# Another way to turn 32 columns of x0: VectorE instead of TensorE in a cross-network kernel, and fewer, larger loads

## The chip, the cores and the metric

The kernel runs on one core of one Trainium2 chip. The metric is device time in microseconds (us) for one execution, as the median of several runs; lower is better. A profile is one further execution, recorded by the hardware profiler. Its "span" is the stretch from the first to the last recorded instruction, and the execution's own time is a little longer than that.

The engines are named as the profile names them: PE is TensorE (matmuls), PEld its weight loads, DVE is VectorE, ACT is ScalarE, POOL is GpSimd, SP is SyncE, which only issues DMAs. ACTq and SPq are the DMA issues of ACT and SP.

## The reference

```
x0: (4096, 416) bf16,  ws: (6, 416, 416) bf16,  bs: (6, 416) bf16

def reference(x0, ws, bs):
    x = x0
    for l in range(ws.shape[0]):
        x = x0 * (x @ ws[l] + bs[l]) + x
    return x
```

Six layers, each a matmul of 4096 x 416 with 416 x 416, a bias, an elementwise product with x0 and a sum with the layer's input.

## The kernel before

**Layout.** Layers 0 to 4 work on transposed data: features lie on the 128 partitions, rows of the batch on the free axis. The 416 features are three blocks of 128 (`XM`, index `m` or `k`) and a remainder of 32. The 4096 batch rows are two halves (`s` = 0, 1) of 2048, and each half is four groups (`g`) of 512 columns. The remainder's 32 features would fill only a quarter of the partitions, so the four groups of a half are stacked: in `XR`, partitions 32g to 32g+31 hold the 32 features of group g, in 512 columns for each half. `XRd` is `XR` with its upper and lower 64 partitions exchanged; layer 0 reads it for the block m = 1 so that neighbouring matmuls use different rows of TensorE.

**Getting x0 there.** The three main blocks come from memory by DMA transposes (L75, `load_x0t`, one for each half and group, eight in all, on SP's queue). The remainder comes as plain rows of 64 bytes. For half 0 four loads on ScalarE's queue (L80) put them into `xrig`, ordered so that four 128 x 128 transposes on TensorE (L155, against the identity) give the stacked form in PSUM, from where VectorE copies it to `XR` and `XRd` (L158). For half 1 one load on SP's queue (L84) fetches them into `xrem`, GpSimd copies them into the order that `xrig` needs (L132), and TensorE and VectorE do the same as for half 0, with the spare bank of the tile `pr` as target.

**The order around it.** SP issues, one after the other: the x0 transposes of half 0, that of half 1's group 0, `xrem` (L84, called at L114), the other three of half 1, then the weights of layers 1 to 5, the batch rows of x0 for the last layer (`X0rows`, L123, four loads), and the last layer's bias row for four partitions (`bLr`, L125, four loads). ScalarE's queue issues the weights of layer 0, the biases, the `xrig` loads and the remainder's weights of layer 0 (`WR`, L87). ScalarE then copies those weights to further partitions (L108) and begins the activations.

**Layer 0** is `first_layer(s)`, half 0 and then half 1. TensorE's matmuls of the main blocks are L212, those of the remainder rows L219 (into the same sums), those that make the remainder's own output L191 and L196. Each block's two groups of 512 columns share a PSUM tile of two banks; four such tiles exist, and ScalarE frees one when it has read it. `ew_main` is: ScalarE adds the bias while it reads PSUM (L163), VectorE multiplies by x0 (L164) and adds the layer's input (L167). `ew_rem` does the same for the remainder (L171, L172, L173). `x0_rem(1, ...)` is called between half 0's `mm_rem` and the elementwise work on half 0's second pair of groups.

**Layers 1 to 4** are the loop at L280 (matmuls L179, L185, L191, L196, the same elementwise work). **Layer 5** computes with the batch rows on the partitions (L325, L331, L334): ScalarE takes the sum out of PSUM (L352), VectorE multiplies by `X0rows` (L353) and adds (L342), and the result is stored (L343).

A planner of the framework lays out each engine's instructions in the order of a planned time and inserts the waits. `tc.keep_in_program_order(ins)` ties one instruction behind the instruction that was written before it for the same engine.

Of the kernel before, what the change touches and what calls it, by code (L numbers as in the profile page):

```python
# [11 lines left out]
BF16 = mybir.dt.bfloat16  # L12
# [4 lines left out]
def kernel(  # L17
# [7 lines left out]
    nc = tc.nc  # L25
    B, D = x0.shape
    L = ws.shape[0]
    P = 128
    NK = 3
    R = D - NK * P  # L30
    assert R == 32 and B == 4096 and D == 416 and L >= 2
    NS = 2
    NG = 4
    CW = 512
    SW = NG * CW
    NBT = B // P
    LL = L - 1

    const = ctx.enter_context(tc.tile_pool(name="const", bufs=1))
    big = ctx.enter_context(tc.tile_pool(name="big", bufs=1))  # L40
# [4 lines left out]
    x0_v = x0.rearrange("(bt p) d -> p bt d", p=P)  # L45
    out_v = out.rearrange("(bt p) d -> p bt d", p=P)

    ident = const.tile([P, P], BF16)
# [6 lines left out]
    bLr = const.tile([P, D], BF16)  # L55
    bM = const.tile([P, NK, L], FP32)
    bR = const.tile([P, L], FP32)
    X0rows = big.tile([P, NBT, D], BF16)
    XLrows = big.tile([P, NBT, D], BF16)
    scrR = [big.tile([P, 4, P], BF16, name=f"scrR{s}") for s in range(NS)]  # L60
    xrem = big.tile([P, 16, R], BF16)
    xrig = big.tile([P, NS, 4, P], BF16)
    XRd = big.tile([P, NS * CW], BF16)
    XM = [big.tile([P, NK, B], BF16, name=f"XM{i}") for i in range(3)]
    XR = [big.tile([P, NS * CW], BF16, name=f"XR{i}") for i in range(3)]

    def col0(s, g):
        return SW * s + CW * g

    def load_wm(eng, l):  # L70
        eng.dma_start(WM[:, l], ws[l, 0:NK * P, :].rearrange("(k p) n -> p k n", p=P))

    def load_x0t(s, g):
        c0 = col0(s, g)
        nc.sync.dma_start_transpose(out=XM[0][:, :, c0:c0 + CW], in_=x0[c0:c0 + CW, 0:NK * P])  # L75

    def load_xrem0():
        with nc.allow_non_contiguous_dma(reason="64B row segments"):
            for i in range(4):
                nc.scalar.dma_start(xrig[:, 0, i, :].rearrange("p (g r) -> p g r", g=NG), x0_v[:, i:16:4, NK * P:D])  # L80

    def load_xrem1():
        with nc.allow_non_contiguous_dma(reason="64B row segments"):
            nc.sync.dma_start(xrem[:], x0_v[:, 16:32, NK * P:D])  # L84

    def load_wr0():
        nc.scalar.dma_start(WR[0:R, 0, :], ws[0, NK * P:D, :])  # L87
# [12 lines left out]
    nc.scalar.dma_start(bsb[:], bs[:, :])  # L100
    load_x0t(0, 1)
    load_xrem0()
    load_wr0()
    nc.scalar.activation(dz[:, 1:2], dz[:, 0:1], ACT.Identity, bias=dz[:, 0:1], scale=1.0)  # L104
    for g in range(1, NG):
        dst, src = WR[32 * g:32 * g + 32, 0, :], WR[0:R, 0, :]
# [4 lines left out]
    for g in range(2, NG):  # L111
        load_x0t(0, g)
    load_x0t(1, 0)
    load_xrem1()  # L114
    for g in range(1, NG):
        load_x0t(1, g)
    load_wm(nc.sync, 1)
# [1 line left out]
        load_wr(nc.sync, g, 1, L)  # L119
    for l in range(2, L):  # L120
        load_wm(nc.sync, l)
    for q in range(4):
        nc.sync.dma_start(X0rows[:, 8 * q:8 * q + 8, :], x0_v[:, 8 * q:8 * q + 8, :])  # L123
    for g in range(NG):
        nc.sync.dma_start(bLr[32 * g:32 * g + 1, :], bs[LL:LL + 1, :])  # L125

    def fill_wd(l0, l1):
        for g in range(NG):
            nc.gpsimd.tensor_copy(WD[32 * g:32 * g + 32, l0:l1, g, :], WR[32 * g:32 * g + 32, l0:l1, NK * P:D])

    fill_wd(0, 1)
    nc.gpsimd.tensor_copy(xrig[:, 1].rearrange("p i (g r) -> p i g r", g=NG), xrem[:].rearrange("p (g i) r -> p i g r", g=NG))  # L132
    fill_wd(1, L)

    wps = psum.tile([P, CW], FP32, tag="ps", name="wps")
# [14 lines left out]
        nc.vector.tensor_copy(bM[:], pb[:, 0:NK, 0:L])  # L150
        nc.vector.tensor_copy(bR[:], pb[:, 3, 0:L])

    def x0_rem(s, tpr):
        for i in range(4):
            nc.tensor.transpose(tpr[:, 128 * i:128 * i + 128], xrig[:, s, i, :], ident[:])  # L155
        for dst, src in ((slice(0, P), slice(0, P)), (slice(64, P), slice(0, 64)), (slice(0, 64), slice(64, P))):
            to = XR[0] if dst == src else XRd
            nc.vector.tensor_copy(to[dst, CW * s:CW * s + CW], tpr[src])  # L158

    def ew_main(l, s, m, h, pt, cur, nxt, pin=False):  # L160
        c0 = col0(s, 2 * h)
        t = tpool.tile([P, 2 * CW], BF16, name="t")
        nc.scalar.activation(t[:], pt[:].rearrange("p a b -> p (a b)"), ACT.Identity, bias=bM[:, m, l:l + 1], scale=1.0)  # L163
        prod = nc.vector.tensor_tensor(out=t[:], in0=t[:], in1=XM[0][:, m, c0:c0 + 2 * CW], op=ALU.mult)  # L164
        if pin:
            tc.keep_in_program_order(prod)
        nc.vector.tensor_tensor(out=nxt[:, m, c0:c0 + 2 * CW], in0=t[:], in1=cur[:, m, c0:c0 + 2 * CW], op=ALU.add)  # L167

    def ew_rem(l, s, pr, curR, nxtR):
        tr = tpool.tile([P, 2 * CW], BF16, name="t")  # L170
        nc.scalar.activation(tr[:, 0:CW], pr, ACT.Identity, bias=bR[:, l:l + 1], scale=1.0)  # L171
        nc.vector.tensor_tensor(out=tr[:, 0:CW], in0=tr[:, 0:CW], in1=XR[0][:, CW * s:CW * s + CW], op=ALU.mult)  # L172
        nc.vector.tensor_tensor(out=nxtR[:, CW * s:CW * s + CW], in0=tr[:, 0:CW], in1=curR[:, CW * s:CW * s + CW], op=ALU.add)  # L173
# [15 lines left out]
    def mm_rem(l, s, pr, cur, curR):  # L189
        for g in range(NG):  # L190
            nc.tensor.matmul(pr[32 * g:32 * g + 32, :], lhsT=WD[:, l, g, :], rhs=curR[:, CW * s:CW * s + CW],  # L191
                             start=True, stop=False, tile_position=(0, 32 * g))
        for k in range(NK):
            for g in range(NG):
                c0 = col0(s, g)
                nc.tensor.matmul(pr[32 * g:32 * g + 32, :], lhsT=WM[:, l, k, NK * P:D], rhs=cur[:, k, c0:c0 + CW],  # L196
                      start=False, stop=(k == NK - 1), tile_position=(0, 32 * g))
# [8 lines left out]
    def first_layer(s):  # L206
        cur, curR, nxt, nxtR = XM[0], XR[0], XM[1], XR[1]

        def full(pt, m, h, gl, after_row):
            c0 = col0(s, 2 * h + gl)  # L210
            for k in range(NK):
                nc.tensor.matmul(pt[:, gl, :], lhsT=WM[:, 0, k, 128 * m:128 * m + 128], rhs=cur[:, k, c0:c0 + CW],  # L212
                                 start=(k == 0 and not after_row), stop=(k == NK - 1 and after_row))

        def row(pt, m, h, opens):
            for gl in range(2):
                rg = 32 * ((2 * h + gl) ^ (2 if m == 1 else 0))
                src = XRd if m == 1 else curR
                nc.tensor.matmul(pt[:, gl, :], lhsT=WR[rg:rg + 32, 0, 128 * m:128 * m + 128],  # L219
                                 rhs=src[rg:rg + 32, CW * s:CW * s + CW],  # L220
                                 start=opens, stop=not opens, tile_position=(rg, 0))

        def ph(m):
            return psum.tile([P, 2, CW], FP32, tag="ps", name=f"ph{m}")

        pa = [ph(m) for m in range(NK)]
        if s == 0:
            for m in range(NK):
                full(pa[m], m, 0, 0, False)
            tp0 = psum.tile([P, CW], BF16, tag="ps", name="tpr")  # L230
            x0_rem(0, tp0[:])
            for m in range(NK):
                full(pa[m], m, 0, 1, False)
        else:
            for m in range(NK):
                for gl in range(2):
                    full(pa[m], m, 0, gl, False)
        pb = [ph(0)]
        row(pa[0], 0, 0, False)
        row(pb[0], 0, 1, True)  # L240
        row(pa[2], 2, 0, False)
        row(pa[1], 1, 0, False)
        for m in range(NK):
            ew_main(0, s, m, 0, pa[m], cur, nxt)
        for m in range(NK):
            if m:
                pb.append(ph(m))
            for gl in range(2):
                full(pb[m], m, 1, gl, m == 0)
        row(pb[1], 1, 1, False)  # L250
        row(pb[2], 2, 1, False)
        pr = psum.tile([P, 2, CW], FP32, tag="ps", name="pr")
        mm_rem(0, s, pr[:, 0, :], cur, curR)
        if s == 0:
            x0_rem(1, pr[:, 1, :].bitcast(BF16)[:, 0:CW])
        for m in range(NK):
            ew_main(0, s, m, 1, pb[m], cur, nxt, pin=(s == 0))
        ew_rem(0, s, pr[:, 0, :], curR, nxtR)
# [3 lines left out]
    for s in range(NS):  # L262
        first_layer(s)
# [147 lines left out]
```

## Time and profile before

| | us |
|---|---|
| median of 3 runs | 130.65 (130.53 to 130.75) |
| the profiled execution's own time | 130.58 |
| its span | 128.8 |

| engine | busy us | share of the span | instructions |
|---|---|---|---|
| PE | 123.6 | 96% | 1691 |
| DVE | 106.7 | 83% | 195 |
| ACT | 86.9 | 67% | 99 |
| POOL | 6.2 | 5% | 18 |

The granted TensorE clock is 1.00 throughout. The DMA engines are busy in the first 40 us (x0 and the weights come in) and in the last 28 us (results go out).

How to read what follows. A row of the timeline is: start in us, length in us, engine, line, operation, what it writes and reads, how many; in brackets the engine's idle time just before it and what ended it. Rows of the same kind are merged. Matmuls overlap, so their length in the profile (0.38 us for 512 columns) is longer than the distance from one start to the next (0.216 us); starts are the surer reading. A row of the chain of waits is: start, length, and the work that the end of the execution goes back to at that moment.

### The profile page before, as it was taken

How to read it: one execution, taken by the hardware profiler on the slowest of the kernel's cores; microseconds unless marked ns; L12 is line 12 of the kernel's file. 1: busy time of each engine (PE TensorE's matmuls, PEld its weight loads, DVE VectorE, ACT ScalarE, POOL GpSimd, SP SyncE). 2: the span in 40 equal slices, each digit the busy share in tenths (PEclk: the TensorE clock that was granted, in tenths of full speed). 3: DMA queues.
4: the chain of work that ended last, by engine and by line, in shares of the span. 5: the costliest groups of instructions: out<-in, count | busy, mean ns of one | idle time of the engine just before them, and what ended most of it. 6: DMA issues, size and time to landing. Idle time of an engine off the chain costs nothing.

```text
span 128.8 us, 3973 instructions
## 1 busy us (share of the span) xinstructions
PE 123.6 (96%) x1691; PEld 55.1 (43%) x1691; DVE 106.7 (83%) x195; ACT 86.9 (67%) x99; POOL 6.2 (5%) x18
## 2 busy tenths in 40 slices
PE   7999999999999999999999999999999999999960
PEld 3343443344545444434444544444444445445420
DVE  0023989999999898989898989898989899898991
ACT  0138873887848667848668848668858896569670
POOL 4004300600000000000000000000000000000000
PEclk9999999999999999999999999999999999999999
DMA  4999999999990000000000000000297999985754
GB/s 95 244 231 207 163 153 264 253 328 333 336 291 9 5 0 8 0 0 5 0 5 0 5 0 5 0 5 0 45 163 169 119 237 191 217 261 186 235 178 138
DMA packets 42102, 16.37 MB, mean 127 GB/s; under 512 B 30906, under 2 KB 42084, under 8 KB 42084
## 3 DMA queue, kind: packets, MB, share of 16 engines
q1 hardware_dynamic: 39368, 15.53, 53.9%
q10 hardware_dynamic: 2716, 0.59, 2.5%
q8 instruction: 13, 0.21, 0.7%
q14 instruction: 5, 0.04, 0.1%
HBM read 6.15 MB, written 3.41 MB: 74 GB/s over the span
## 4 chain that ended last, share of the span: by engine, by line
PE 89%; DVE 6%; issue 2%; ACT 1%; DVEq 0%
PE pt L179 49%; PE ph L212 13%; PE py L325 8%; PE pt L185 5%; PE pr L196 5%; PE wps L139 4%; DVE t L353 4%; DVE o L342 2%; PE pr L191 2%; PE ph L219 1%; PE py L331 1%; PE py L334 1%; ACT t L352 1%; PE tpr L155 0%; PE pr L155 0%
## 5 line engine op out<-in xcount | busy, mean ns | idle before, releaser
L179 PE MATMUL pt<-XM,WM 128*32 128x512 bf16 x1152 | 65.2, 379 | 0.0
L163 ACT ACTIVATE t<-pt,bM 128x1024 bf16<-128x1024 f32 x48 | 49.6, 1115 | 18.5 <-PE pt L185 18.5
L164 DVE TENSOR_TENSOR t<-t,XM 128x1024 bf16<-128x1024 bf16 x60 | 41.4, 690 | 5.2 <-ACT t L163 5.2
L167 DVE TENSOR_TENSOR XM<-t,XM 128x1024 bf16<-128x1024 bf16 x60 | 41.8, 697 | 3.4
L179 PEld LDWEIGHTS <-WM 128*32 128x32 bf16 x1152 | 29.7, 97 | 33.8 <-issue 5.1
L352 ACT CAST t<-py 128x416 bf16<-128x416 f32 (+1 forms) x23 | 14.8, 642 | 4.8 <-PE py L325 2.6
L325 PE MATMUL py<-WM,XM 128*128 128x416 bf16 x96 | 17.7, 340 | 0.0
L212 PE MATMUL ph<-XM,WM 128*128 128x512 bf16 x72 | 16.5, 381 | 0.0
L163 ACT ACTIVATE t<-ph,bM 128x1024 bf16<-128x1024 f32 x12 | 12.5, 1114 | 3.4 <-PE ph L219 3.4
L325 PEld LDWEIGHTS <-XM 128*128 128x128 bf16 x96 | 9.0, 98 | 8.5 <-issue 1.4
L353 DVE TENSOR_TENSOR t<-t,X0rows 128x416 bf16<-128x416 bf16 (+1 forms) x23 | 10.4, 457 | 1.2 <-ACT t L352 1.2
L342 DVE TENSOR_TENSOR o<-t,XLrows 128x416 bf16<-128x416 bf16 (+1 forms) x23 | 10.4, 456 | 0.0
L212 PEld LDWEIGHTS <-WM 128*128 128x128 bf16 x72 | 6.7, 98 | 8.4 <-issue 1.1
L171 ACT ACTIVATE t<-pr,bR 128x512 bf16<-128x512 f32 x10 | 6.4, 685 | 2.7 <-PE pr L196 2.1
L196 PE MATMUL pr<-XM,WM 128*32 128x512 bf16 x120 | 8.2, 379 | 0.0
L185 PE MATMUL pt<-XR,WR 32*128 32x512 bf16 x96 | 7.3, 379 | 0.0
L139 PE MATMUL wps<-const-bfloat16-1.0 128*128 128x512 bf16 (+1 forms) x12 | 4.9, 592 | 0.8 <-PEq L395 0.8
L104 ACT ACT_TABLE_LOAD x1 | 1.3, 1283 | 6.0 <-DMA XM<-in_x_dram 6.0
L173 DVE TENSOR_TENSOR XR<-t,XR 128x512 bf16<-128x512 bf16 x10 | 4.2, 425 | 0.7
L196 PEld LDWEIGHTS <-WM 128*32 128x32 bf16 x120 | 3.2, 97 | 3.0
L150 DVE CAST bM<-pb 128x18 f32<-128x18 bf16 x1 | 0.2, 177 | 5.1 <-PE pb L149 5.1
L172 DVE TENSOR_TENSOR t<-t,XR 128x512 bf16<-128x512 bf16 x10 | 4.2, 420 | 0.0
(38 smaller groups left out, 33.5 us busy)
## 6 DMA issues: line engine op xcount, KB each, us to landing
X0rows<-in_x_dram SPq DMA_DIRECT2D x4, 832.0 KB, 11.5
out_dram<-o SPq DMA_DIRECT2D x9, 208.0 KB, 2.5
WM<-in_ws_dram SPq DMA_DIRECT2D x5, 312.0 KB
out_dram<-o SPq DMA_DIRECT2D x13, 104.0 KB, 1.9
WR<-in_ws_dram SPq DMA_DIRECT2D x4, 130.0 KB, 4.1
WM<-in_ws_dram ACTq DMA_DIRECT2D x1, 312.0 KB
XM<-in_x_dram SPq DMA_TRANSPOSE x8, 4.9
xrig<-in_x_dram ACTq DMA_DIRECT2D x4, 32.0 KB, 4.2
```

The source lines that it names most:

```text
L139: nc.tensor.matmul(wps[:, 0:cols], lhsT=warm[:, 0:P], rhs=warm[:, 0:cols], start=True, stop=True)
L163: nc.scalar.activation(t[:], pt[:].rearrange("p a b -> p (a b)"), ACT.Identity, bias=bM[:, m, l:l + 1], scale=1.0)
L164: prod = nc.vector.tensor_tensor(out=t[:], in0=t[:], in1=XM[0][:, m, c0:c0 + 2 * CW], op=ALU.mult)
L167: nc.vector.tensor_tensor(out=nxt[:, m, c0:c0 + 2 * CW], in0=t[:], in1=cur[:, m, c0:c0 + 2 * CW], op=ALU.add)
L179: nc.tensor.matmul(pts[g // 2][32 * q:32 * q + 32, g % 2, :], lhsT=WM[:, l, k, 128 * m + 32 * q:128 * m + 32 * q + 32], rhs=cur[:, k, c0:c ...
L185: nc.tensor.matmul(pts[g // 2][:, g % 2, :], lhsT=WR[32 * g:32 * g + 32, l, 128 * m:128 * m + 128], rhs=curR[32 * g:32 * g + 32, CW * s:CW ...
L196: nc.tensor.matmul(pr[32 * g:32 * g + 32, :], lhsT=WM[:, l, k, NK * P:D], rhs=cur[:, k, c0:c0 + CW], start=False, stop=(k == NK - 1), tile ...
L212: nc.tensor.matmul(pt[:, gl, :], lhsT=WM[:, 0, k, 128 * m:128 * m + 128], rhs=cur[:, k, c0:c0 + CW], start=(k == 0 and not after_row), sto ...
L325: nc.tensor.matmul(py[:, 0:D], lhsT=cur[:, k, q_cols(q, g)], rhs=WM[:, l, k, :], start=((not closes) and k == 0), stop=(closes and k == NK ...
L342: tc.keep_in_program_order(nc.vector.tensor_tensor(out=o, in0=t, in1=xl, op=ALU.add))
L352: nc.scalar.copy(tv, src)
L353: tc.keep_in_program_order(nc.vector.tensor_tensor(out=tv, in0=tv, in1=X0rows[:, b, :], op=ALU.mult))
```

## The change

The remainder of half 1 no longer goes through GpSimd and TensorE. Its load takes the rows in another order (sixteen neighbouring rows on each partition), so that one VectorE transpose in blocks of 32 x 32 writes the stacked form straight to `XR`; two copies inside the on-chip memory make `XRd`. The load moves from SP's queue to ScalarE's and is called after half 0's remainder is done: a small memset of `xrem` on VectorE, tied behind the copies of half 0, must be over before the load may write there, and the load itself is tied behind what stands before it on ScalarE's queue. `xrig` serves half 0 alone. `X0rows` comes in one load instead of four, `bLr` in one load with a repeated source instead of four.

```
+    def pin(ins):
+        tc.keep_in_program_order(ins)
...
     def load_xrem1():
+        pin(nc.vector.memset(xrem[:, 0, 0:1], 0.0))
         with nc.allow_non_contiguous_dma(reason="64B row segments"):
-            nc.sync.dma_start(xrem[:], x0_v[:, 16:32, NK * P:D])
+            pin(nc.scalar.dma_start(xrem[:], x0[SW:2 * SW, NK * P:D].rearrange("(p t) r -> p t r", p=P)))
...
     load_x0t(1, 0)
-    load_xrem1()
     for g in range(1, NG):
         load_x0t(1, g)
...
-    for q in range(4):
-        nc.sync.dma_start(X0rows[:, 8 * q:8 * q + 8, :], x0_v[:, 8 * q:8 * q + 8, :])
-    for g in range(NG):
-        nc.sync.dma_start(bLr[32 * g:32 * g + 1, :], bs[LL:LL + 1, :])
+    nc.sync.dma_start(X0rows[:], x0_v)
+    nc.sync.dma_start(bLr[0:P:32, :], bs[LL:LL + 1, :].to_broadcast([NG, D]))
...
-    nc.gpsimd.tensor_copy(xrig[:, 1].rearrange("p i (g r) -> p i g r", g=NG), xrem[:].rearrange("p (g i) r -> p i g r", g=NG))
...
-    def x0_rem(s, tpr):
+    def x0_rem0(tpr):
         for i in range(4):
-            nc.tensor.transpose(tpr[:, 128 * i:128 * i + 128], xrig[:, s, i, :], ident[:])
+            nc.tensor.transpose(tpr[:, 128 * i:128 * i + 128], xrig[:, i, :], ident[:])
         for dst, src in ((slice(0, P), slice(0, P)), (slice(64, P), slice(0, 64)), (slice(0, 64), slice(64, P))):
             to = XR[0] if dst == src else XRd
-            nc.vector.tensor_copy(to[dst, CW * s:CW * s + CW], tpr[src])
+            pin(nc.vector.tensor_copy(to[dst, 0:CW], tpr[src]))
+        load_xrem1()
+
+    def x0_rem1():
+        pin(nc.vector.transpose(XR[0][:, CW:2 * CW].rearrange("p (j t) -> p t j", t=16), xrem[:]))
+        for dst, src in ((slice(64, P), slice(0, 64)), (slice(0, 64), slice(64, P))):
+            pin(nc.vector.tensor_copy(XRd[dst, CW:2 * CW], XR[0][src, CW:2 * CW]))
...
         if s == 0:
-            x0_rem(1, pr[:, 1, :].bitcast(BF16)[:, 0:CW])
+            x0_rem1()
```

More of the change, by code (lines that the diff above doesn't have):

```diff
@@ L61 @@
     xrem = big.tile([P, 16, R], BF16)
-    xrig = big.tile([P, NS, 4, P], BF16)
+    xrig = big.tile([P, 4, P], BF16)
     XRd = big.tile([P, NS * CW], BF16)
@@ L79, in load_xrem0 @@
             for i in range(4):
-                nc.scalar.dma_start(xrig[:, 0, i, :].rearrange("p (g r) -> p g r", g=NG), x0_v[:, i:16:4, NK * P:D])
+                nc.scalar.dma_start(xrig[:, i, :].rearrange("p (g r) -> p g r", g=NG), x0_v[:, i:16:4, NK * P:D])
     def load_xrem1():
+        pin(nc.vector.memset(xrem[:, 0, 0:1], 0.0))
         with nc.allow_non_contiguous_dma(reason="64B row segments"):
-            nc.sync.dma_start(xrem[:], x0_v[:, 16:32, NK * P:D])
+            pin(nc.scalar.dma_start(xrem[:], x0[SW:2 * SW, NK * P:D].rearrange("(p t) r -> p t r", p=P)))
     def load_wr0():
@@ L230, in first_layer @@
             tp0 = psum.tile([P, CW], BF16, tag="ps", name="tpr")
-            x0_rem(0, tp0[:])
+            x0_rem0(tp0[:])
             for m in range(NK):
```

## The prediction

> **What bounds the kernel now.** I read the chain of waits first. It is TensorE without a break from 0.77 us to 115.65 us of the span, and after that a short ScalarE step and VectorE to the end:
>
> ```profile
> 15.41 0.33 PE ph L219 x4
> 15.73 0.33 PE pr L191 x4
> 16.06 0.65 PE pr L196 x12
> 16.71 0.33 PE pr L155 x4
> 17.04 3.88 PE ph L212 x18
> ...
> 115.65 0.02 issue
> 115.67 0.86 ACT t L352
> ```
>
> The columns are start, length and work. The four L155 matmuls are the second half's transposes, inside the unbroken run. The table of who waited for whom, asked of PE alone, has one row, 0.8 us before the first matmul. So a microsecond taken out of PE's queue after 16 us moves everything behind it, and a delay on another engine costs only what is over its margin against PE. The chain's 0.33 are modelled ends; the starts stand in the timeline of PE around the transposes:
>
> ```profile
> 16.32 0.39 PE L196 MATMUL pr<-XM,WM 128*32 128x512 bf16 x4
> 16.64 0.40 PE L155 MATMUL pr<-ident,xrig 128*128 128x128 bf16 x4
> 16.88 0.81 PE L212 MATMUL ph<-XM,WM 128*128 128x512 bf16 x3
> ```
>
> From the first transpose's start to that of the next useful matmul it is 16.88 - 16.64 = 0.24 us (0.235 with the trace's third digit). Third come the other queues' timelines, for the margins:
>
> ```profile
> 5.64 0.34 ACTq L87 DMA_DIRECT2D WR<-in_ws_dram  x1
> 6.00 1.28 ACT L104 ACT_TABLE_LOAD   x1 [6.00 <-DMA XM<-in_x_dram]
> 9.66 1.10 ACT L108 COPY WR<-WR 32x416 bf16<-32x416 bf16 x2 [2.07 <-DMA WR<-in_ws_dram]
> 11.09 1.11 ACT L163 ACTIVATE t<-ph,bM 128x1024 bf16<-128x1024 f32 x1 [0.33 <-PE ph L219]
> ```
>
> ```profile
> 10.31 0.58 SPq L84 DMA_DIRECT2D xrem<-in_x_dram  x1
> 10.95 6.79 SPq L75 DMA_TRANSPOSE XM<-in_x_dram  x3
> 17.78 1.41 SPq L71 DMA_DIRECT2D WM<-in_ws_dram  x1
> ```
>
> ```profile
> 14.90 0.68 DVE L164 TENSOR_TENSOR t<-t,XM 128x1024 bf16<-128x1024 bf16 x1
> 15.62 0.98 DVE L167 TENSOR_TENSOR XM<-t,XM 128x1024 bf16<-128x1024 bf16 x1
> 17.08 0.42 DVE L158 COPY XR<-pr 128x512 bf16<-128x512 bf16 x1 [0.48 <-PE pr L155]
> 17.54 0.86 DVE L158 COPY XRd<-pr 64x512 bf16<-64x512 bf16 x2
> 18.31 0.68 DVE L164 TENSOR_TENSOR t<-t,XM 128x1024 bf16<-128x1024 bf16 x1
> ```
>
> ACTq and SPq rows are DMA issues. The first ACTIVATE waits for PE, not the reverse; VectorE waits 0.48 us for the transposes.
>
> **PE: four transposes fewer.** The change of tile shape from L196 costs 0.31 us before the transposes (16.333 to 16.644) and none after them; I take it to stay, now in front of L212. Gain 0.235. Bounds: if that gap shrinks to the 0.205 seen from L196 to L179 (26.386 to 26.591) the gain is 0.235 + 0.106 = 0.34; if it grows by as much, 0.13. Among the rows on TensorE L196 to L155 is the nearest, both next tiles being 128*128, so 0.235.
>
> The row's own durations are 0.22 us each, overlapped. [...]
>
> **VectorE.** Removed: three copies from PSUM, 0.42 + 0.86, with the wait of 0.48 ahead of them. Added: one transpose of 128x512, two copies of 64x512 from SBUF, one memset of one column. No row shows a VectorE transpose. Nearest rows of that size: the PSUM copy 0.42 below, GpSimd's regrouping copy of 128x512 at 1.06 above; I take 0.7. The two copies are at most 0.42 each. The memset is about the 0.06 of L93's. The third L167, 0.98 long only while GpSimd's copy of xrig runs (15.00 to 16.06; otherwise 0.69), ends near 16.31. So x0_rem1 would run 16.3 to 17.9 instead of 17.08 to 18.39. Who needs it: PE's L219 rows, at 20.86 now and 20.62 then. Cost nothing, hidden by 2.7 us of PE's own L212 run; with 1.06 it is still hidden. ScalarE's L171, which now waits 0.59 us for the last XRd copy, is freed too; it leads to nothing late.
>
> [...]
>
> **GpSimd** loses the L132 copy of 1.06 us; its next work waits 6.99 us for WR anyway: nothing.
>
> **SP's queue** loses 0.58 us of xrem's issue ahead of three x0 loads, the weights of layers 1 to 5 and X0rows. The trace's completion events give their landings: XM for (1,0) 13.53, xrem 14.88, (1,1) 16.96, (1,2) 19.81, (1,3) 21.15, WM of layer 1 22.23. PE needs them at 16.88, -, 17.53, 21.40, 22.06 and 26.4. No wait exists, so earlier landings gain nothing. PE's 0.24 lead cuts the smallest margin, of (1,1), from 0.57 to 0.33; but today all of xrem stands ahead of that load, and on another queue it can at most be in the same place, so I expect (1,1) no later than now.
>
> **X0rows in one issue, bLr in one.** They occupy SP from 23.28 to 34.51; used at 107.4 and 105.0. SP has nothing else to issue until the XLrows transposes near 98. Worth nothing, cover 70 us; without the cover, the issue time saved is at most the two rows' 11 us.
>
> **The load on ScalarE's queue.** Behind it on that engine stand all L163 activations, whose first frees PSUM for PE. The load waits for the memset, behind the XRd copies that end at 9.98: ready at 10.05 to 10.1. An event wait of L163 was already taken at 9.67, while both L108 copies (to 10.76) were still to run, so the sequencer passes them and can issue at 10.1. Issue length: L80's four were 0.37 to 0.66, xrem's on SP 0.58. So 10.7, before 11.09: no delay. If it can only start after the copies, 10.76 + 0.66 = 11.4, a delay of 0.33. PE needs the first activation's end, now 12.20, at its seventh L212:
>
> ```profile
> 11.35 1.68 PE L212 MATMUL ph<-XM,WM 128*128 128x512 bf16 x7
> ```
>
> The seventh starts at 11.35 + 1.68 - 0.38 = 12.65. Margin 0.45. Hidden both ways.
>
> **Sum.** Profiled execution 130.58 with a span of 128.8 and 1.8 around it: 130.58 - 0.235 = 130.35, span 128.57. That execution lies 0.07 under the median 130.65, so the median becomes 130.41, 0.18% less. What this kernel's measurement can tell from no change is about 0.2%, 0.26 us.
>
> **Rivals.**
>
> (A) *ScalarE is held by the load (slower).* Decides from a delay of 0.45 us of the first activation, and is slower than before from 0.45 + 0.235 = 0.69. Two ways to reach it. The compiled program gives its loads eight semaphores in turn, and each load waits for the one eight places earlier: L87's load was issued at 5.64 when the first XM had landed at 5.61, and the row of L104 names that XM. If xrem's load comes 17th or 18th in the compiler's order it waits for loads landed by 9.64 and nothing happens; as 19th it waits for XM (0,3), landed at 11.50: issue to 12.1, first activation 1.0 late, PE loses 1.0 - 0.45 = 0.55, net +0.3: 130.96. As 20th, for XM (1,0) at 13.53: net about +2.3: 132.95. Or the issue is as slow as SP's longest, 3.08 us (the first of the three at 10.95): 10.1 + 3.08 = 13.2, 2.1 late, net 2.1 - 0.45 - 0.235 = +1.4: 132.05. For: the load is traced after x0_rem0, when SP is well ahead. Against: in the old program's order the XRd copies stand between the loads that become 15th (the last x0 transpose) and 17th or 18th once xrem's is out of SP's row, so 19th would need it later by one whole load; and L87 took 0.34 beside SP's busy queue. Chance 0.15, two thirds of it at the small price.
>
> (B) *The new traffic delays an x0 load (slower).* XM (0,3) lands at 11.50 and PE takes it at 12.01; xrem's packets now come 1.3 us earlier than they did. If it loses what xrem took between landings, 14.88 - 13.53 = 1.35, PE waits 1.35 - 0.5 = 0.85 and the net is +0.6: 131.25. Against: its issue is over at 8.87. Chance 0.08.
>
> (C) *No gain:* the old rhythm returns behind some wait that the margins above don't show; 130.65. No PE wait speaks for it. Chance 0.06.
>
> (D) *More than forecast:* the tile-change gap shrinks as well, 0.34: 130.31; chance 0.16. That the transpose changes nothing in PE's queue is excluded, as the four matmuls are gone.
>
> **How the numbers follow.** Forecast 0.55, A 0.15, B 0.08, C 0.06, D 0.16. The forecast of 130.41 lies just short of the bound at 130.39; with a spread of 0.1 for medians of three I give it 0.29 faster, 0.26 same. Faster: 0.29 + 0.16 = 0.45. Same: 0.26 + 0.06 = 0.32. Slower: 0.23. The forecast's own range is 130.28 to 130.52 (gain 0.13 to 0.34, widened by little); the whole range reaches down to D's 130.31 less 0.09 for spread, 130.22, and up over A's small price to 131.00, leaving out A's large prices and B.
>
> **What would show it.** Right: PE's first L212 of the second half starts at 16.64 with no wait of PE on anything; VectorE's transpose ends before 18.4; ScalarE's first L163 still starts at 11.1; the chain lacks L155's second group. Wrong: a PE wait on ACT near 12.65 or on XM near 12.0 or 17.3; an ACTq issue over 1 us at 10 to 14; a transpose so late that L219 rows wait at 20.6.

## The result

| | us | ratio to before |
|---|---|---|
| before, median of 6 runs | 130.56 (130.49 to 130.75) | |
| after, median of 6 runs | 131.44 (131.17 to 131.75) | 1.0063, 95% interval 1.0048 to 1.0078 |
| after, the profiled execution | 131.53 | |
| its span | 129.7 | |

The changed kernel is 0.88 us slower, not 0.24 us faster. The profiled execution of before took 130.58 with a span of 128.8, so the two profiles differ by 0.95 us and hold the loss.

**TensorE does what was forecast.** In the timeline of PE of the changed kernel (start, length, engine, line, operation) the second half's main blocks follow the remainder's output with no transposes between:

```profile
15.83 0.40 PE L197 MATMUL pr<-XR,WD 128*32 128x512 bf16 x4
16.05 0.82 PE L202 MATMUL pr<-XM,WM 128*32 128x512 bf16 x12
16.81 1.47 PE L218 MATMUL ph<-XM,WM 128*128 128x512 bf16 x6
```

From L202's last start (16.494) to L218's first (16.806) it is 0.31 us, the gap that stood ahead of the transposes before.

**VectorE's transpose is over three times as long as taken, and the load on ScalarE's queue does not hold ScalarE.** The timelines of VectorE and of ScalarE:

```profile
15.80 0.69 DVE L173 TENSOR_TENSOR XM<-t,XM 128x1024 bf16<-128x1024 bf16 x1
16.55 2.37 DVE L162 STREAM_TRANSPOSE XR<-xrem 128x512 bf16<-128x512 bf16 x1
18.95 0.61 DVE L164 COPY XRd<-XR 64x512 bf16<-64x512 bf16 x2
19.59 0.69 DVE L170 TENSOR_TENSOR t<-t,XM 128x1024 bf16<-128x1024 bf16 x1
```

```profile
9.82 0.54 ACT L112 COPY WR<-WR 32x416 bf16<-32x416 bf16 x1 [2.04 <-DMA WR<-in_ws_dram]
10.23 0.63 ACTq L88 DMA_DIRECT2D xrem<-in_x_dram  x1
10.38 0.54 ACT L112 COPY WR<-WR 32x416 bf16<-32x416 bf16 x1
11.27 2.12 ACT L169 ACTIVATE t<-ph,bM 128x1024 bf16<-128x1024 f32 x2 [0.35 <-PE ph L225]
```

The transpose takes 2.37 us and the remainder is ready at 19.56 (18.95 + 0.61), which is still before PE's L225 rows at 20.80. The load is issued in 0.63 us beside the copies and lands at 16.53 by its completion records, 0.02 us before the transpose starts, for which VectorE stood idle 0.06 us. The first ACTIVATE waits for PE, as before.

**Up to the last VectorE operation the two kernels take the same time.** The chain of waits of the changed kernel ends with the same steps as before, and the first of them stands 0.02 us earlier than in the old profile (115.67):

```profile
110.83 4.33 PE py L331 x24
...
115.65 0.86 ACT t L358
```

VectorE's last operation ends at 126.18 (125.52 + 0.66 for the last two) in the new profile, at 126.19 in the old. So the 0.22 us that TensorE saves are gone by then. Half 0's second group of main blocks (L212, now L218) starts at 8.81 instead of 8.62, which leaves TensorE 0.16 us behind until the saving, and another 0.05 go from layer 1 on, 0.03 of them in a wait for VectorE (below). In both kernels the second group starts 0.04 us after the second x0 load of half 0 has landed (8.58 before, 8.76 after).

All of the difference of the two profiles lies behind VectorE's last operation, with the stores. The timelines of SP and ScalarE from 125.75 us on show the last issues, first of before:

```profile
125.41 0.87 SPq L343 DMA_DIRECT2D out_dram<-o  x2
126.22 0.37 ACTq L343 DMA_DIRECT2D out_dram<-o  x1
```

and of after:

```profile
126.21 0.39 ACTq L349 DMA_DIRECT2D out_dram<-o  x1
126.22 0.33 SPq L349 DMA_DIRECT2D out_dram<-o  x1
```

Before, SP's last two issues ran together from 125.41; by the records the last began at 125.93. After, SP issues its last store at 126.22, 0.29 us later. And what it issues takes longer to land. The view of the DMAs from 126 to 130 us in forty slices (busy tenths, then GB/s), of before:

```profile
DMA  9606995079999950300000000000000000000000
GB/s 374 183 9 208 374 333 142 17 250 333 325 300 366 366 167 17 82 0 0 0 0 0 0 0 0 0 0 0 0 0 0 0 0 0 0 0 0 0 0 0
```

and of after, with its list of issues (queue, count, KB each, median us from issue to landing):

```profile
DMA  1179930000299999930000000000000000000000
GB/s 33 42 250 358 325 100 0 0 0 0 75 356 349 333 350 308 291 84 25 17 25 0 0 0 0 0 0 0 0 0 0 0 0 0 0 0 0 0 0 0
...
out_dram<-o ACTq DMA_DIRECT2D x1, 104.0 KB, 2.5
out_dram<-o SPq DMA_DIRECT2D x1, 104.0 KB, 2.2
```

A slice is 0.1 us. Before, the last two stores move from 126.8 on, at up to 366 GB/s, and are done by 127.6 (the 82 behind them is a transfer of 8192 bytes of instructions at 127.60). After, the DMA engines stand still from 126.6 to 127.0 and then move the last two stores, but from 127.8 to 128.1 a thin stream of 17 to 25 GB/s is left: a small part is still moving when the rest is done. Each store reports 16 completions; by the records, for each of the last two stores one of the 16 comes late, 0.45 and 0.51 us after the fifteenth. The last completion is at 128.70 instead of 127.97: +0.74. It is ScalarE's store's in both kernels; the fifteenth of that store's completions comes at 128.19 instead of 127.92, so 0.27 us of the 0.74 are all of the data coming later, and 0.47 the one late completion.

The remaining 0.17 us lie between the last completion and the end of the span: 1.01 us after, 0.84 before. SP's table of waits shows it as another pattern of the last waits (total, times, longest), of before and of after:

```profile
SPq L406 <- DMA out_dram<-o: 1.4, 4, 0.5
```

```profile
SPq L412 <- DMA out_dram<-o: 2.1, 1, 2.1
```

The single waits of SP show where they lie. After the last completion SP still takes three more waits, at 128.764, 128.828 and 128.890, before it goes on at 128.955; before, the wait for the last store is the last of the row, and SP goes on at 128.047, 0.08 us after the completion.

0.74 + 0.17 is the whole difference of the spans, 0.91.

**Why SP is late.** The records of SP's instructions hold no wait that explains it. But they hold one idle stretch that is the same in both kernels by its place in the sequence, not by its time:

```
SP's instructions, counted from 0: start in us, idle time just before it
before  78 wait   123.455  0.045      after  78 store  125.347  0.177
before  79 store  123.913  0.441      after  79 wait   126.147  0.467
before  80 wait   124.301  0.056      after  80 store  126.222  0.058
```

Number 79 comes 0.44 to 0.47 us after its predecessor, where the steps beside it take 0.05 to 0.18. The change takes seven instructions out of SP's stream ahead of the stores (one load of `xrem`, three of `X0rows`, three of `bLr`), so the pause that stood ahead of the fifth-last SP store now stands ahead of the last one. The trace also holds transfers of 8192 bytes of the kind "instruction", one of them 0.6 to 1.0 us after the pause (124.55 before, 127.12 after). And the two stores behind the pause of before have a late completion too (0.36 and 0.32 us after the fifteenth), only that three more stores follow there and hide it.

This gave the theory for the experiments: *SP runs out of a block of instructions at this place; it pauses, and the fetch that follows delays one DMA engine's part of the stores that are on the way. The removed loads matter only by their number.* The rivals: the new path of the remainder (VectorE late, another order of loads) costs the time; or the two merged loads do, by what they move.

### The profile page after: what moved, and what is told of

The parts are those of the page before. It is cut to its first block, busy times and chain, and to the rows that moved or that the text cites. A ratio compares the mean times of both kernels' runs of the same rounds, so it can differ in the third digit from the quotient of the medians.

```text
span 129.7 us, 3956 instructions
## 1 busy us (share of the span) xinstructions
PE 122.9 (95%) x1687; PEld 55.3 (43%) x1687; DVE 108.2 (83%) x196; ACT 86.6 (67%) x99; POOL 4.7 (4%) x17
## 4 chain that ended last, share of the span: by engine, by line
PE 83%; DVE 6%; DMA 4%; ACTq 2%; issue 2%; ACT 1%; DVEq 0%
PE pt L185 49%; PE ph L218 11%; PE py L331 8%; PE pt L191 5%; PE pr L202 5%; DMA xrig<-in_x_dram 4%; DVE t L359 4%; DVE o L348 2%; PE pr L197 2%; PE ph L225 1%; PE py L337 1%; ACTq L83 1%; PE py L340 1%; ACT t L358 1%; ACTq L104 1%
## 5 line engine op out<-in xcount | busy, mean ns | idle before, releaser
L218 PE MATMUL ph<-XM,WM 128*128 128x512 bf16 x72 | 16.4, 380 | 0.4 <-DMA XM<-in_x_dram 0.4
L218 PEld LDWEIGHTS <-WM 128*128 128x128 bf16 x72 | 6.8, 97 | 9.1 <-issue 1.7
L202 PE MATMUL pr<-XM,WM 128*32 128x512 bf16 x120 | 8.2, 379 | 0.0
L139 PE MATMUL wps<-const-bfloat16-1.0 128*128 128x512 bf16 (+1 forms) x12 | 4.4, 545 | 0.8 <-PEq L401 0.8
L202 PEld LDWEIGHTS <-WM 128*32 128x32 bf16 x120 | 3.3, 97 | 2.9
```

## The experiments

"no-op" is an instruction on SP that does nothing, put behind the `bLr` loads, 70 us ahead of the stores:

```
+    for _ in range(7):
+        tc.keep_in_program_order(nc.sync.nop(hint='pad', nofuse=True))
```

### The four that tell the causes apart

*nop7*: the changed kernel with seven no-ops, so that SP has as many instructions as before.

> The changed kernel with seven empty instructions added to SP's queue behind the load of bLr, where SP is idle until 91 us; loads, transposes and stores are untouched. Theory F (the changed kernel has seven SP instructions fewer, and a pause before the 80th recorded SP instruction, where its next block of instructions begins, has moved from the fifth-last SP store to the last one): the pause returns to the fifth-last store, the last two stores land near 127.7 to 128.0 of the span, and the time falls from 131.44 to about 130.5 (130.56 of before, less 0.235 of PE, plus up to 0.19 because SP's last waits meet the last store early in their order). Rival M (one large X0rows load and one bLr load cost by themselves): no change, 131.4. Rival R (the remainder's new path costs): no change, 131.4.

*mergeonly*: the kernel before, with the two merged loads alone.

```
-    for q in range(4):
-        nc.sync.dma_start(X0rows[:, 8 * q:8 * q + 8, :], x0_v[:, 8 * q:8 * q + 8, :])
-    for g in range(NG):
-        nc.sync.dma_start(bLr[32 * g:32 * g + 1, :], bs[LL:LL + 1, :])
+    nc.sync.dma_start(X0rows[:], x0_v)
+    nc.sync.dma_start(bLr[0:P:32, :], bs[LL:LL + 1, :].to_broadcast([NG, D]))
```

> The kernel before with X0rows and bLr in one load each and nothing else changed; SP has six instructions fewer. Theory F: the pause falls on the second-last SP store, the last stores are late by 0.3 to 0.9, and PE gains nothing: 131.0 to 131.5. Rival M: about 131.4. Rival R: 130.56, as the remainder's path is the old one.

*unmerged*: the changed kernel with the eight old loads (the reverse of that edit).

> The changed kernel with X0rows and bLr loaded in four pieces each again; SP then has one instruction fewer than in the kernel before. Theory F: the pause falls one instruction later than in the kernel before, at the fourth-last SP store, and the last store is undisturbed: 130.56 - 0.235 = 130.33. Rival M: 130.3 too. Rival R: 131.2 or more, since only the loads are undone.

*before_nop121*: the kernel before with 121 no-ops, so that the next block would end near the last store if a block has 128 instructions (8192 bytes would then be 64 for each).

> The kernel before with 121 empty instructions on SP behind the loads of bLr, where SP is idle for 57 us; nothing else is changed. The trace shows instruction fetches of 8192 bytes, so a block would be 128 instructions of 64 bytes; 121 more put the next block's start where the changed kernel has the first, ahead of the last SP store. Theory F with blocks of 128: slower than before by 0.6 to 1.0, 131.2 to 131.5, by empty instructions alone. Theory F with blocks of 256: the old pause moves away from the end and none comes there, 130.56 or a little less. Rivals M and R: 130.56.

| kernel | SP instructions | the pause (idle before no. 79) | median us | ratio, 95% interval |
|---|---|---|---|---|
| before | 98 | ahead of the fifth-last SP store | 130.56 | |
| after | 91 | ahead of the last | 131.44 | 1.0063 (1.0048 to 1.0078) |
| mergeonly | 92 | ahead of the second-last | 131.43 | 1.0066 (1.0050 to 1.0081) |
| nop7 | 98 | ahead of the fifth-last | 130.63 | 1.0005 (0.9996 to 1.0015) |
| unmerged | 97 | ahead of the fourth-last | 130.74 | 1.0005 (0.9990 to 1.0020) |
| before_nop121 | 219 | among the no-ops, and again 128 later, ahead of the last store | 130.91 | 1.0028 (1.0017 to 1.0040) |

Seven instructions that do nothing take away some 0.8 us. That is the decisive run: everything the change does to the data is still there in nop7. mergeonly has a loss of the same size without the new path of the remainder, so that path is not the cause; and nop7 has both merged loads without the loss, so what they move is not the cause either. The view of the DMAs of nop7, same stretch:

```profile
GB/s 42 158 341 358 200 58 58 275 333 316 250 358 349 183 17 0 0 0 0 0 0 0 0 0 0 0 0 0 0 0 0 0 0 0 0 0 0 0 0 0
...
out_dram<-o SPq DMA_DIRECT2D x1, 104.0 KB, 1.7
out_dram<-o ACTq DMA_DIRECT2D x1, 104.0 KB, 1.7
```

The thin stream at the end is gone (one slice of 17 GB/s is left), and both last stores land 1.7 us after their issue. In before_nop121 the second pause is there (last SP store issued at 126.02 instead of 125.93) and the last completion is at 128.18, 0.21 us later than before; the kernel is slower by 0.35 us, less than after's 0.88. So the position by number, 79 and 79 + 128, is confirmed; that a block of instructions ends there stays an inference, from this distance and from the transfers of 8192 instruction bytes. The size of the loss is not confirmed: 131.2 to 131.5 was expected. In this profile the late completions are only 0.13 and 0.17 us behind the fifteenth; why they are shorter than in after is open.

unmerged was expected at 130.33 and took 130.74, with runs from 130.32 to 131.18. In its profile the second group of main blocks starts at 8.81 again, which takes back TensorE's 0.22 us; the last completion is at 128.00, as in before.

### The pause out of the way, and the pause behind the last store

*before_nop13*, *unmerged_nop14* and *nop20* put the pause near 120 us, eleven SP stores ahead of the end, in the kernel before, in unmerged and in the changed kernel.

> The kernel before with 13 empty SP instructions behind the loads of bLr. They move the pause from the fifth-last SP store back by 13 instructions, to about 120 us, where every later store still has time to catch up. Theory F: if the pause cost the kernel before anything, at most the 0.1 to 0.2 by which its last stores' landings look slow, it is gone: 130.4 to 130.57. Rival: it cost nothing there, 130.57.

> The remainder's new path alone (X0rows and bLr in four loads each), with 14 empty SP instructions, so that the pause is at the same store as in before_nop13. The two differ by the remainder's path alone. If PE's 0.235 us arrives at the end: 0.2 less than before_nop13, 130.2 to 130.35. If the new path loses it again at the start (the second group of layer 0 began 0.1 to 0.2 us later in three profiles of the new path than in three of the old): equal to before_nop13 within 0.1.

> The whole change with 20 empty SP instructions, the pause again at the same store as in before_nop13 and unmerged_nop14; 58 DMAs instead of 64. Theory F: 130.4 to 130.6, no longer slower than before. The last store signals the second of the five semaphore waits that end SP's stream, and not the last as with 64 DMAs, so about 0.19 us (three more waits of 0.064) slower than unmerged_nop14; if that order does not matter, equal to it.

| kernel | the pause, us | median us | ratio, 95% interval |
|---|---|---|---|
| before_nop13 | 120.26 | 130.55 | 1.0003 (0.9991 to 1.0014) |
| nop20 | 120.41 | 130.51 | 0.9997 (0.9987 to 1.0007) |
| unmerged_nop14 | 120.75 | 130.42 | 0.9996 (0.9980 to 1.0012) |

before_nop13 shows that the kernel before loses nothing by its own pause. nop20 shows that the changed kernel loses nothing any more, and still gains nothing that can be told: it keeps the other order of the last waits, 1.01 us from the last completion to the end. Of the fourteen profiles of this study the nine kernels with 64 loads and stores in all have 0.83 to 0.84 there, the five with 58 (after, nop7, nop20, mergeonly, store2act) 1.006 to 1.02. The loads and stores signal eight semaphores in turn, and SP waits for those in a fixed order at the end: by the records, with 64 the last store's is in the last wait of the row, with 58 in the second of five, and the other three are then passed one by one behind it, about 0.064 us each. No run changed this order alone. unmerged_nop14 was expected at 130.2 to 130.35 and took 130.42: four of its twelve runs lie from 130.75 to 131.16, its profile (130.92) among them.

*store2act* moves the second-last store to ScalarE's queue too, so that SP's stream ends ahead of the pause:

```
-            ew(q + u // 4, u % 4, n, tiles[tl][:, a:a + n, 0:D], nc.scalar if q + 2 == NQ and u == 7 else nc.sync)
+            ew(q + u // 4, u % 4, n, tiles[tl][:, a:a + n, 0:D], nc.scalar if q + 2 == NQ and u >= 6 else nc.sync)
```

> The whole change, with the second-last store issued from ScalarE's queue instead of SP's. SP has two instructions fewer, and its pause falls behind its last store, on waits that wait anyway. Theory F: the last SP store is undisturbed, 130.4 to 130.7. If instead fewer SP instructions always make it worse, or the loads themselves cost: 131.4 or more.

131.53 us, 1.0071 (1.0050 to 1.0091). A miss, and a useful one. The pause did move behind SP's last store (to 126.45, ahead of SP's waits for the end), and no store is issued late for it; the timeline of ScalarE and its list of issues:

```profile
126.23 0.87 ACTq L349 DMA_DIRECT2D out_dram<-o  x2
```

```profile
out_dram<-o ACTq DMA_DIRECT2D x2, 104.0 KB, 2.3
```

Both stores still land 2.4 and 2.2 us after their issue instead of 1.7, each with a completion that comes late (last one 128.89), while the instruction transfer runs at 127.08 for 0.63 us. So the late completion does not need a late issue by SP, and it comes on either queue. (In this profile VectorE's last operation also ends 0.31 us later than in after, from a second group that starts at 9.13.) The profile of after agrees: its last completion belongs to ScalarE's store, which was issued on time (126.21, before 126.22). SP's late issue adds its part there: SP's store is issued 0.02 us behind ScalarE's and no longer 0.29 us ahead of it, so that the two move together, and that fits the 0.27 us by which the fifteenth completion is late; no run shows it alone.

Nor does it need SP's pause. In the new path's profiles another transfer of 8192 instruction bytes runs near 124 to 125 us, and in the eight of them where SP's pause is more than 1 us away a store on the way has its last completion 0.25 to 0.57 us late (nop20: transfer at 124.95, pause at 120.41, the store of 124.21 is 0.29 late). Stores that follow hide it there. It does not happen at every transfer: before has one at 127.60, and its last store's last completion is 0.04 us behind the fifteenth. So the late completion goes with the fetch; a pause of SP is not needed for it. That the fetch's bytes and the late part of the store share one DMA engine fits one late completion out of 16; the records don't show which engine a packet used, so this last step is argued, not shown.

### VectorE's transpose

nop20 and unmerged_nop14 showed a second loss, in layer 1. The timelines of PE and of VectorE of nop20:

```profile
32.42 0.82 PE L204 MATMUL pr<-XM,WM 128*32 128x512 bf16 x12
33.27 0.40 PE L199 MATMUL pr<-XR,WD 128*32 128x512 bf16 x4
```

```profile
32.80 0.42 DVE L181 TENSOR_TENSOR XR<-t,XR 128x512 bf16<-128x512 bf16 x1
```

From L204's last start (32.862) to L199's first (33.274) it is 0.41 us, where 0.21 is usual: L199 reads the XR that L181 writes until 33.22. VectorE is late by what the transpose took too long 16 us earlier. Four kernels followed.

*tr_contig*: unmerged_nop14, with the transpose's blocks written one behind the other. Its columns come out in another order, so half 1's remainder is a permuted one in this kernel; the amount of work is the same.

```
-        pin(nc.vector.transpose(XR[0][:, CW:2 * CW].rearrange("p (j t) -> p t j", t=16), xrem[:]))
+        pin(nc.vector.transpose(XR[0][:, CW:2 * CW].rearrange("p (t j) -> p t j", t=16), xrem[:]))
```

> The version unmerged_nop14 with one other edit: VectorE's transpose writes its 32-column blocks one after the other (contiguous output) instead of every 16th column, so the columns of half 1's remainder come out in another order. Theory: the 2.37 us of the transpose come from the 2-byte elements written 32 bytes apart; it then takes 0.7 to 1.3 us, x0_rem1 ends over 1 us earlier, VectorE is no longer behind in layer 1, the wait of TensorE's L199 group on VectorE near 33 us (starts 0.455 us apart in unmerged_nop14, 0.21 without the wait) goes, and the time falls by 0.1 to 0.25 us to about 130.2 to 130.3. Rival: the duration is the transpose's own, whatever the order of its output: 2.2 to 2.5 us, the wait stays, 130.4 as in unmerged_nop14.

130.36 us, 0.9986 (0.9977 to 0.9995). The timelines of VectorE and PE:

```profile
16.14 0.70 DVE L166 STREAM_TRANSPOSE XR<-xrem 128x512 bf16<-128x512 bf16 x1
16.88 0.61 DVE L168 COPY XRd<-XR 64x512 bf16<-64x512 bf16 x2
```

```profile
32.35 0.82 PE L206 MATMUL pr<-XM,WM 128*32 128x512 bf16 x12
33.00 0.39 PE L201 MATMUL pr<-XR,WD 128*32 128x512 bf16 x4
```

The same transpose takes 0.70 us instead of 2.37 when neighbouring outputs are neighbours in memory and not 32 bytes apart; that part of the theory holds. There is no wait in layer 1 (33.00 follows 32.35 + 0.82 - 0.38 by 0.21), but this profile would not have shown one with the slow transpose either, as `xrem` had landed early, at 15.88 (see below). What the short transpose gives is margin: the XR that L201 reads is ready at 30.98, 2.0 us before its start, where unmerged_nop20 below has 0.35. The time is 0.06 us under unmerged_nop14's; 0.1 to 0.25 was expected.

*xrig2* and *unmerged_nop20* ask where the scatter of the changed kernels comes from.

```
-    xrig = big.tile([P, 4, P], BF16)
+    xrig = big.tile([P, NS, 4, P], BF16)
```

> unmerged_nop14 with xrig at its old size (twice as large, the second half unused). Theory: the later start of half 0's second group of main blocks (8.62 us in the mean of four profiles with the old path, 8.84 in six with the new one) is scatter of the first loads' landings: 8.6 to 9.0 us here too, and the time 130.3 to 130.5. Rival: it is the place of the tiles behind xrig in the on-chip memory: with the old size it comes back to 8.55 to 8.7, and the time falls to 130.2.

> unmerged with 20 no-ops instead of 14 on SP. Theory (SP's pause at its 80th recorded instruction, away from the last stores, costs nothing): as unmerged_nop14, 130.35 to 130.5, and the second cluster of unmerged_nop14's times (130.75 to 131.16 in 4 of 12 runs) is the landing of the first loads, so that it can come back here. Rival: those times come from the place of the pause; six instructions earlier they stay away or come in all runs.

xrig2: 130.44 us, 0.9993 (0.9981 to 1.0005); its second group of main blocks starts at 8.83 us, later than in the old kernels (8.55 to 8.73), so the old size of `xrig` alone does not bring it back; this is one profile. unmerged_nop20: 130.40 us, 0.9989 (0.9980 to 0.9998), all eleven runs from 130.26 to 130.57. **This version is faster than both kernels**, but barely clear of noise: 0.17 us under before, 0.03 to 0.26 by the interval, one of twelve variants. Runs above 130.75 as in unmerged_nop14 did not occur; whether the place of the pause or the landing of the first loads made them is not decided. In its profile the transpose started at 16.33 and the wait in layer 1 did not occur; in xrig2, where `xrem` landed later and the transpose started at 16.77, it did (0.47 from start to start). All eight profiles with the slow transpose agree: in the five where VectorE stood idle for `xrem` (0.06 to 0.27 us) TensorE waits in layer 1 (0.03 to 0.26 us), in the three where VectorE did not stand idle, TensorE does not wait. So with the slow transpose the landing of `xrem` decides from run to run.

*contig4* tries for a right order and a contiguous transpose together: four loads on ScalarE's queue, two of them early, and the transpose written as in tr_contig.

```
...
+                c0 = col0(1, g)
+                pin(nc.scalar.dma_start(xrem[32 * g:32 * g + 32], x0[c0:c0 + CW, NK * P:D].rearrange("(t j) r -> j t r", j=32)))
...
```

> Half 1's remainder by four loads on ScalarE's queue, one for each group, so that VectorE's transpose can write contiguously and in the right order: two issued in ScalarE's idle time before 9.7 us, two after its copies of WR; the last bias row in one load and 23 no-ops on SP, so that the counts of loads (64) and of SP's instructions stay as in unmerged_nop20. Theory: the transpose takes 0.70 us as in tr_contig, no wait on VectorE near 33 us, SP's pause far ahead of the last stores: 130.3 to 130.4, below both kernels. Rival: the earlier packets of the two first loads delay the transposed loads of x0 that layer 0's first half waits for, or the two later issues (0.6 us each) hold ScalarE's first activation past its margin of 0.45 us: 130.6 to 131.2, with a gap of TensorE near 9 or 12 us.

130.63 us, 1.0000 (0.9991 to 1.0009): no gain. The transpose takes 0.70 us, but PE loses at the front what it gains. The timelines of ScalarE and PE:

```profile
9.96 0.54 ACT L114 COPY WR<-WR 32x416 bf16<-32x416 bf16 x1 [2.17 <-DMA WR<-in_ws_dram]
10.49 0.32 ACTq L89 DMA_DIRECT2D xrem<-in_x_dram  x1
10.53 0.54 ACT L114 COPY WR<-WR 32x416 bf16<-32x416 bf16 x1
```

```profile
10.70 0.81 PE L230 MATMUL ph<-XR,WR 32*128 32x512 bf16 x6
11.34 0.38 PE L230 MATMUL ph<-XRd,WR 32*128 32x512 bf16 x2
11.65 0.82 PE L223 MATMUL ph<-XM,WM 128*128 128x512 bf16 x2
```

The weights `WR` land at 9.96, the second copy of them ends at 11.06, and the rows L230 stretch over 0.96 us (10.695 to 11.651) where the other thirteen profiles have 0.60 to 0.77. Taken alone 9.96 is not late (the others have 9.53 to 10.18), but against the x0 load that starts the second group it is: the copies start 1.34 us after that load has landed, in the others 0.99 to 1.16. The early `xrem` packets run ahead of or beside the load of `WR`; that they delay it fits, but no run took them away alone.

## Why the prediction was wrong

**The step that failed** is "X0rows in one issue, bLr in one": "Worth nothing, cover 70 us". For the time of the loads that is right: the two issues now take 0.49 and 9.99 us on SP, hidden like the old ones. But the step counted only what an instruction does and not that it stands in SP's stream. Six of the seven instructions that the change removes there are these; mergeonly, with these six alone, has a loss of the same size (131.43, 0.87 over before), and nop7, with seven empty ones in their place, has none (130.63). The term was not zero but about +0.74 us by the profiles of before and after, plus 0.17 for the order of the last waits, which goes with 58 loads and stores in place of 64. With the 0.22 us of TensorE's gain that did not reach the end, these make up about the 1.14 us by which the span (129.71) lies over the forecast 128.57.

**PE: right.** From the first matmul behind half 0's last remainder rows (15.66 in before) to half 1's first ones (20.86) it is 5.195 us in all four profiles with the old path and 4.971 or 4.972 in all ten with the new one: 0.224 gained, 0.235 forecast, with the gap of 0.31 moved ahead of L218 as taken. That it would move "everything behind it" to the end did not hold in after: the later landing of the second group's x0 load puts TensorE 0.16 us back, 0.05 go from layer 1 on, and the prediction had a term for neither. For the same reason the second half's first L218 starts at 16.81 and not at the forecast 16.64. unmerged_nop20, with the new path, the old eight loads and the no-ops, takes 130.40, where the forecast was 130.41; the agreement to 0.01 is luck in part, as its runs scatter from 130.26 to 130.57.

**VectorE: mis-sized, and its cover was not complete.** The transpose was taken as 0.7 us, from rows between 0.42 and 1.06, and measured 2.37; 0.70 is what it takes with a contiguous output. No row of the old trace had an access of that stride, and the bound of 1.06 should have been wider for it. The step also had no time for the landing of `xrem` by ScalarE's queue: 16.53 in after, 6.3 us after its issue, where the old load took 4.6. The transpose ends at 18.92, past the 18.4 given as a sign of being right. Its cover against the L225 rows held (19.56 against 20.80). What the step missed is the next one: VectorE stays late by the difference, and some 14 us later TensorE can wait for it, by up to 0.26 us (0.47 from start to start in xrig2 where 0.21 is usual), more than the whole gain.

**ScalarE's load, rivals A and B: right not to take them.** The load was issued at 10.23 in 0.63 us, no earlier load held it, and the first ACTIVATE still waited for PE. No x0 load of half 1 was waited for. The slower side was foreseen with a chance of 0.23, but for these mechanisms, and none of the four rivals was the one that came.

**GpSimd, SP's earlier issues: right.** Nothing waits for either: no row of PE's table of waits in after names GpSimd or a load of half 1 (its one row on x0 is half 0's first load, 0.4 us ahead of 5.85).

**Left open:** in all fourteen profiles the second group of main blocks starts 0.04 us after the second x0 load of half 0 has landed; why that load lands at 8.49 to 9.09 us in the ten with the new path and at 8.51 to 8.69 in the four with the old is not known. In the kernels other than contig4 the load of `xrem` is issued only afterwards, one profile with the old size of `xrig` (xrig2) is late too, and chance was not excluded. Also open is which packets delay the one late completion, and why some transfers of instructions delay none.

## What to carry to other kernels

An instruction that is fully hidden can still cost time by being one more or one fewer in its queue's stream (here six fewer cost 0.87 us in mergeonly, and seven empty ones took 0.81 away in nop7). When a change removes or adds instructions on an engine that issues the last stores, look where the idle stretch of that stream falls, in the old and the new count, and pad with no-ops if it falls on the last stores. When two profiles agree up to the last compute operation and differ behind it, compare issue, landing and final waits of the last stores before looking for a cause in the edit's data. A VectorE operation that is hidden against its own reader must also be followed to the next point where the engine has no slack (here some 14 us on, where TensorE waits up to 0.26 us).

## What the runs showed of the hardware

- SP pauses 0.42 to 0.47 us ahead of its instruction number 79 (counted from 0 among the recorded ones) in all fourteen profiles, and with 219 instructions again at 207, for 0.36; transfers of 8192 instruction bytes follow within about 1 us.
- Stores on the way during a transfer of 8192 instruction bytes can get one of their 16 completions late, by 0.45 to 0.79 us in after, mergeonly and store2act: 2.2 to 2.6 us from issue to landing instead of 1.7, on ScalarE's queue too, and 0.25 to 0.57 us where SP did not pause near it. Not every such transfer does this: beside the one at 127.60 in before, the last store's last completion is 0.04 us behind the fifteenth.
- The end of the span comes 0.83 to 0.84 or 1.01 to 1.02 us after the last completion, with 64 and with 58 loads and stores on the eight semaphores that they signal in turn.
- VectorE's transpose of 128x512 bf16 in blocks of 32 x 32 takes 0.70 us with contiguous output and 2.37 us with elements 32 bytes apart.
